# Mixed products of the third contraction tile through the seven-product scheme, low parts of the softmax by pairs of tiles, four heads over eight query tiles

## The chip, the cores and the metric

The kernel runs on one core of one Trainium2 chip. The metric is the device time of one execution in microseconds (us). Three runs before the change took 2610.6 us in the median (2606.59 to 2613.32). The kernel writes its results in float32 and works on float16 pairs: every float32 operand is kept as a high part and a low part (the rest), and a product of two such operands is taken as high x high + high x low + low x high.

## The reference

The reference adds three things: the input x (1 x 2048 x 448, float32), a 16-head attention block of the normalized x, and a mixture of 8 experts in which all 8 are used for every row (so no row is left out, and the gates are a softmax over all 8 logits).

```python
xn = _layernorm(x, axis=-1)
return x + _A_ref(xn, A_wqkv, A_wo) + _B_ref(xn, B_w_gate, B_w1, B_w2)
...
    qkv = (lambda x, *d: x.transpose(*d))((x @ wqkv).reshape(B, S, 3, H, Dh), 2, 0, 3, 1, 4)
    scores = jnp.einsum("bhqd,bhkd->bhqk", q, k) * (Dh ** -0.5)
    p = _softmax(scores, axis=-1)
    o = jnp.einsum("bhqk,bhkd->bhqd", p, v)
...
    for e in range(E):
        w = (gates * mask).sum(-1, keepdims=True)
        h = _silu(xf @ w1[e]) @ w2[e]
        out = out + w * h
```

Here S = 2048, D = 448, H = 16, Dh = 28, E = 8, and the hidden width F of an expert is 1792.

## The kernel before

**Three streams and a planner.** A first stage (phase0, the first 110 us or so) normalizes x, turns it, and makes Q, K, V and the gates. Then two streams run beside each other to the end: the experts (function moe) and the attention (function attention). Nothing is issued directly: every piece of work is a job for one engine, with an estimated duration, a due value v, and the buffers that it reads and writes. Plan.run plays the jobs through with those estimates and issues on each engine, of the jobs that could start, the one with the smallest (v, seq). What comes out is one fixed order of instructions for each engine; on the chip the engines keep that order and wait for each other by semaphores. A buffer tag with n buffers is handed out in the order in which the buffers were asked for.

**Experts.** The 1792 hidden columns of an expert are cut into groups of 5, 5 and 4 tiles of 128: 24 groups in all. The 2048 rows are 4 chunks of 512. For one group and one chunk, unit() makes four hidden tiles (two pairs f = 0, 1; the two pairs are the q of the loops) for two half chunks i = 0, 1 of 256 columns. There are 24 x 4 = 96 units. The contraction over 448 rows has tiles k = 0, 1, 2 of 128 rows and a rest of 64 (k = 3). Tiles 0 and 1 go through a scheme with seven products in place of eight (strassen(), L1084 to L1096): the 2 x 2 blocks of the weights (A) and of x (B) are combined into sums (S1 to S4 in the buffer wa, T1 to T4 in xt). Each product takes three matmuls for each pair (high x high, high x low, low x high), so 7 x 2 x 3 = 42 matmuls of 256 columns. Tile 2, the lone third tile, and the rest are done directly by plain() (L1098 to L1109), four times a unit, with 8 matmuls each: for each pair high x high, high x low and low x high of tile 2 and one for the rest. tails() (L1111 to L1121) adds 8 matmuls that use 64 rows each. The groups of 5 have one further tile (single(), L1162). The second layer is summed() (L1311).

**Attention.** A step is one head and one tile of 128 query rows: 16 x 16 = 256 steps, ordered by TILES: four heads, and for each four query tiles (NB = 4). load_k, load_v and load_q are called once in four steps. In a step, score() multiplies Q by all 2048 keys in two halves (L1420), VectorE takes the extremes (L1424, mx), ScalarE the exponentials (L1437, pf) and the high parts of p (L1445, ph), VectorE the low parts (L1440, pl). turn() transposes both by DMA on SP's queue (L1458: th, tl). weigh() comes once in four steps: lows_of_p() multiplies the low parts of all four tiles by V (L1492), 16 matmuls that use 32 columns of the array each, four beside each other, over 4 x 128 = 512 columns; highs_of_p() does the high parts (L1499). The buffer tl holds four tiles and exists once (TL = 1), th holds one tile and exists four times. project() multiplies by wo (L1585).

Names in the rows: wc holds the high and low parts of tile 2 and the rest; hr holds the high and low parts of the hidden layer; s5 is a copy of a bank in float32 with a buffer of its own, and t (tag th, three buffers) the hidden tile inside silu().

## Time and profile before

| what | value |
|---|---|
| median of three runs | 2610.6 us (2606.59 to 2613.32) |
| the profiled execution, its own time | 2610.42 us |
| its span, first to last instruction | 2608.6 us |
| TensorE busy (PE) | 2572.0 us, 99% |
| VectorE busy (DVE) | 2328.2 us, 89% |
| ScalarE busy (ACT) | 2065.4 us, 79% |
| GpSimd busy (POOL) | 1370.4 us, 53% |
| packets of the DMA queue that SP feeds | 83.7% of 16 engines' span |
| granted TensorE clock, mean | 0.999 |

The profiled execution lies 0.2 us below the median, and 1.8 us of its time lie outside its span. A matmul of TensorE is drawn from its start to its modelled end, and the next one starts well before that end; so the busy share of PE alone does not tell how densely the matmuls follow each other. The distance from one start to the next does.

### The profile page before, as it was taken

The page shows a single profiled execution, that of the slowest core. Times are in us where ns is not written, and L with a number is a line of the kernel's source. Part 1 is how long each engine was busy: PE and PEld are TensorE (multiplying, and loading weights), DVE is VectorE, ACT ScalarE, POOL GpSimd, SP SyncE. Part 2 cuts the span into 40 slices and gives each one's busy share as a digit, 9 for nine tenths or more (in the row PEclk, how much of TensorE's full clock was granted, in tenths as well). Part 3 has the DMA queues.
Part 4 walks back from the last instruction along what each step waited for, and adds up shares of the span by engine and source line. Part 5 has one row for each costly group of instructions (what it writes and reads, how often), then busy time and mean ns, then how long its engine had stood idle before and what let it go on. Part 6 is the DMA issues. An engine that isn't in the chain of part 4 may idle for free.

```text
span 2608.6 us, 54466 instructions
## 1 busy us (share of the span) xinstructions
PE 2572.0 (99%) x20863; PEld 1612.0 (62%) x20863; DVE 2328.2 (89%) x3127; ACT 2065.4 (79%) x2993; POOL 1370.4 (53%) x1377
## 2 busy tenths in 40 slices
PE   9999999999999999999999999999999999999999
PEld 4466666666666666666665666666666666666666
DVE  9689899988998899988999899898889889998986
ACT  5578878886887888778788888888788887878874
POOL 2365545563655545456455556456455653645633
PEclk9999999999999999999999999999999999999999
DMA  9868979887898899968898888877888888997875
GB/s 264 206 153 167 185 173 189 180 174 168 171 195 172 178 175 202 182 155 178 189 182 179 166 189 187 168 177 177 174 177 190 168 172 180 187 197 162 181 157 136
DMA packets 1262757, 466.94 MB, mean 179 GB/s; under 512 B 1169440, under 2 KB 1218080, under 8 KB 1262496
## 3 DMA queue, kind: packets, MB, share of 16 engines
q1 hardware_dynamic: 1261936, 463.44, 83.7%
q8 instruction: 164, 2.69, 0.5%
q14 instruction: 97, 0.79, 0.1%
q10 hardware_dynamic: 560, 0.02, 0.0%
HBM read 160.09 MB, written 17.35 MB: 68 GB/s over the span
## 4 chain that ended last, share of the span: by engine, by line
PE 73%; DVE 14%; ACT 8%; issue 3%; DMA 3%; SPq 0%; DVEq 0%; ACTq 0%
PE banks L1311 29%; PE banks L1090 13%; PE banks L1106 10%; PE banks L1420 7%; PE banks L1162 5%; DVE mx L1424 4%; DVE pl L1440 3%; PE banks L1499 3%; PE banks L1492 2%; ACT pf L1437 2%; ACT ph L1445 2%; DMA tl<-pl 2%; DVE t L1249 2%; PE banks L1117 2%; DVE acc L1322 1%
## 5 line engine op out<-in xcount | busy, mean ns | idle before, releaser
L1311 PE MATMUL banks<-w,hr 128*128 128x448 f16 x5364 | 1083.2, 353 | 2.1 <-DVE t L1249 1.1
L1255 POOL TENSOR_TENSOR hr<-t,hr 128x512 f16<-128x512 f32 x448 | 606.7, 1368 | 576.6 <-ACT hr L1253 553.0
L1437 ACT ACTIVATE pf<-banks,mx 128x1024 f32<-128x1024 f32 x512 | 568.9, 1111 | 322.6 <-DVE mx L1424 316.9
L1311 PEld LDWEIGHTS <-hr 128*128 128x128 f16 x5364 | 516.3, 98 | 493.2 <-issue 24.0
L1440 DVE SCALAR_TENSOR_TENSOR pl<-pf,ph 128x1024 f16<-128x1024 f32 x512 | 718.2, 1404 | 57.2 <-ACT ph L1445 56.6
L1424 DVE TENSOR_REDUCE mx<-banks 128x1 f32<-128x1024 f32 x512 | 622.4, 1216 | 77.0 <-PE banks L1420 60.3
L1445 ACT ACTIVATE ph<-pf 128x1024 f16<-128x1024 f32 x512 | 539.8, 1055 | 6.2
L1090 PEld LDWEIGHTS <-wa 128*128 128x128 f16 x4032 | 392.4, 98 | 115.9 <-issue 13.7
L1106 PE MATMUL banks<-xs,wc 128*128 128x256 f16 x3072 | 395.2, 272 | 1.0 <-DVE banks L1141 0.7
L1106 PEld LDWEIGHTS <-wc 128*128 128x128 f16 x3072 | 299.3, 98 | 61.7 <-issue 5.0
L1246 ACT ACTIVATE t<-banks,the 128x512 f32<-128x512 f32 x448 | 289.8, 683 | 54.2 <-PE banks L1117 38.7
L1249 DVE SCALAR_TENSOR_TENSOR t<-t,banks 128x512 f32<-128x512 f32 x448 | 291.6, 678 | 36.7 <-ACT t L1246 35.7
L1090 PE MATMUL banks<-xt,wa 128*128 128x256 f16 x2304 | 314.4, 272 | 5.4 <-ACT banks L1131 4.7
L1420 PE MATMUL banks<-K,Q 112*128 112x512 f16 x1024 | 306.3, 380 | 2.8 <-ACT pf L1437 2.6
L1253 ACT ACTIVATE hr<-t 128x512 f16<-128x512 f32 x448 | 267.5, 627 | 18.6 <-DVE t L1249 17.9
L1322 DVE SCALAR_TENSOR_TENSOR acc<-banks,gwe,acc 128x448 f32<-128x448 f32 x383 | 254.7, 674 | 30.5 <-PE banks L1311 29.9
L1090 PE MATMUL banks<-xs,wa 128*128 128x256 f16 x1728 | 235.8, 272 | 0.4 <-DVE acc L1322 0.4
L567 POOL TENSOR_TENSOR wc<-r,wc 128x512 f16<-128x512 f32 x64 | 83.6, 1306 | 208.1 <-ACT wc L563 186.0
L634 POOL TENSOR_TENSOR w<-r,w 128x448 f16<-128x448 f32 x112 | 138.5, 1240 | 100.8 <-ACT w L631 94.7
L1162 PE MATMUL banks<-xs,wc 128*128 128x512 f16 x704 | 164.5, 379 | 1.2 <-DVE t L1249 1.2
L1420 PEld LDWEIGHTS <-Q 112*128 112x128 f16 x1024 | 94.4, 98 | 77.3 <-issue 20.8
L1499 PEld LDWEIGHTS <-th 128*128 128x128 f16 x4096 | 118.6, 96 | 13.9 <-issue 4.7
(174 smaller groups left out, 2343.0 us busy)
## 6 DMA issues: line engine op xcount, KB each, us to landing
xt<-xd SPq DMA_DIRECT2D x71, 512.0 KB
K<-qk SPq DMA_DIRECT2D x512, 56.0 KB
r<-in_B_w_dram SPq DMA_DIRECT2D x16, 1120.0 KB
V<-vs SPq DMA_DIRECT2D x64, 256.0 KB
r<-in_B_w_dram SPq DMA_DIRECT2D x16, 960.0 KB
Q<-qk SPq DMA_DIRECT2D x256, 28.0 KB
r<-in_B_w_dram SPq DMA_DIRECT2D x8, 896.0 KB
r<-in_B_w_dram SPq DMA_DIRECT2D x8, 768.0 KB
```

The costliest lines, as they stand in the source:

```text
L1090: nc.tensor.matmul(bank()[:, q * HC : (q + 1) * HC], w, xx, start=(start and q == 0 and i == 0), stop=True, skip_group_check=True,)
L1106: nc.tensor.matmul(bank()[:, q * HC : (q + 1) * HC], ww, xx, start=False, stop=True, skip_group_check=True,)
L1162: nc.tensor.matmul(z(), rows[:, blk, :], xx, start=(i == 0), stop=(i == NTERM - 1))
L1246: add("ACT", 686, lambda: nc.scalar.activation(t(), z(), AF.Tanh, scale=th_()[:, 0:1]), v, r=[z, (th_, 0)], w=[t])
L1249: lambda: nc.vector.scalar_tensor_tensor(t(), t(), 1.0, z(), op0=ALU.add, op1=ALU.mult),
L1255: add("POOL", 1159, lambda: nc.gpsimd.tensor_tensor(hl(), t(), hh(), ALU.subtract), v, r=[t, hh], w=[hl])
L1311: nc.tensor.matmul(y()[:, 0:D], a, wv, start=(i == 0 and u == 0), stop=(i == g - 1 and u == 2))
L1420: nc.tensor.matmul(b()[:, cs], q()[:, q0 : q0 + P], k()[:, cs], start=True, stop=True)
L1424: nc.vector.tensor_reduce(m()[:, n, j : j + 1], b(), op=ALU.min, axis=AX.X)
L1437: nc.scalar.activation(p(), s(), AF.Exp, bias=m()[:, n, j : j + 1], scale=-1.0)
L1440: nc.vector.scalar_tensor_tensor(l()[:, js], p(), P_SCALE, h()[:, js], op0=ALU.mult, op1=ALU.subtract)
L1445: add("ACT", 1060, lambda: nc.scalar.activation(h()[:, js], p(), AF.Copy, scale=P_SCALE), v, r=[p], w=[(h, j)])
```

## The change

**Third tile.** For each output block, the two mixed products of tile 2 are high_f x low_i + low_f x high_i. That is itself a product of a 2 x 2 block matrix of weights, with rows (high_f, low_f), by a 2 x 2 block matrix of x, with rows (low_i, high_i). The change takes it through the same seven products as tiles 0 and 1: every strassen product gets a fourth matmul for each pair, and plain() keeps only high x high and the rest, 4 matmuls in place of 8. The combined blocks of the weights (four of 128 columns for each pair of tiles, scaled by 1 / 2048 on ScalarE, summed on GpSimd) go into wa, which grows from 14 to 18 tiles of 128; those of x are made once on VectorE (first_two, last_two), stored with the other combinations, and loaded with them. xt is now two halves (q) of 6 x 256 with three buffers in place of 8 x 256 with two.

**Low parts of p.** tl is now a ring of two buffers of one tile each. lows_of_p() runs for a pair of tiles: 16 matmuls over 2 x 128 = 256 columns, twice in four steps, each into a bank of its own, and ScalarE copies each bank.

**Order of the steps.** TILES goes through four heads with eight query tiles each (NH = 8), and K and V are loaded once in eight steps. The output tile ost holds eight query tiles.

**Buffers.** s5 now takes one of the three buffers of tag th; the further tile of a group of 5 has its weights in a tag of its own (wz) with one buffer; ro, u and ohl share one; rwo reuses the buffers of rqk; w2 has 8 buffers in place of 7. The planner's rates stay, except UNIT_NS (78 to 76 half rounds).

```diff
-NB, TL, TH = 4, 1, 4
+NB, NH, TL, TH = 4, 8, 2, 4
...
+        add("ACT", 420, less, v, r=[(wc, 0)], w=third)
+        add("POOL", 1150, crosses, v, r=[(wc, 1), *third], w=[(wa, 4)], steps=2)
+        add("POOL", 1150, more_crosses, v, r=[(wc, 1), *third], w=[(wa, 4)], steps=2)
...
-            s5 = buf("mp", [P, C], F32, f"s5{name}", tag="s5")
+            s5 = buf("mp", [P, C], F32, f"s5{name}", tag="th", bufs=RT)
...
-                        for i, (w, xx) in enumerate(((h, xp[0]), (h, xp[1]), (l, xp[0]))):
+                        xx3 = xp[2] if xc is None else xc
+                        for i, (w, xx) in enumerate(((h, xp[0]), (h, xp[1]), (l, xp[0]), (wx, xx3))):
...
-                        for ww, xx in (
-                            (w[:, 0, 0], xs[:, 2, t[i]]), (w[:, 0, 0], xs[:, 6, t[i]]), (w[:, 1, 0], xs[:, 2, t[i]]),
-                            (w[:, 0, 1], xs[:, 3, t[i]]),
-                        ):
+                        for ww, xx in ((w[:, 0, 0], xs[:, 2, t[i]]), (w[:, 0, 1], xs[:, 3, t[i]])):
...
-            XS_[gi, b] = x = buf("mp", [P, 8, HC], F16, f"xt{gi}_{b}", tag="xt", bufs=2)
+            xt = [buf("mp", [P, 6, HC], F16, f"xt{gi}_{b}_{q}", tag="xt", bufs=3) for q in range(2)]
...
-        TILES = [(4 * k + a, t0 + n) for k in range(H // 4) for t0 in range(0, NT, NB) for a in range(4) for n in range(NB)]
+        TILES = [(4 * k + a, t0 + n) for k in range(H // 4) for t0 in range(0, NT, NH) for a in range(4) for n in range(NH)]
...
-                PT[i] = [], buf("ap", [P, NB, NKT, P], F16, f"tl{i}", tag="tl", bufs=TL)
+                PT[i] = [], []
...
+            tl = buf("tl", [P, NKT * P], F16, f"tl{i}", bufs=TL, tag="tl")
...
-            add("PE", 1052, lows_of_p, v, r=[*((tl, q) for q in range(NB)), vb], w=[zl], more=155)
-            add("ACT", 597, lambda: nc.scalar.activation(lt(), zl(), AF.Copy, scale=1 / SEL), v, r=[zl], w=[lt])
+            for u, zl in enumerate(zls):
+                pair = tls[2 * u : 2 * u + 2]
+                add("PE", 560, lambda zl=zl, pair=pair: lows_of_p(zl, pair), v, r=[*pair, vb], w=[zl], more=155)
...
-                load_k(i, 0, at(i - 2) if i else at(-9))
-                load_k(i, 1, at(i - 1))
-                load_v(i, at(i - 2))
+                if i % NH == 0:
+                    load_k(i, 0, at(i - 2) if i else at(-9))
+                    load_k(i, 1, at(i - 1))
+                    load_v(i, at(i - 2))
```

**How the change moves instructions.** On TensorE before, the share of one pair of tiles (one q) of the first of the seven products, in the middle of the program; wa holds the weights, xs the turned x:

```order
L1090 LDWEIGHTS wa_0_15242
L1090 MATMUL banks<-xs,wa_0_15242 128x256
L1090 LDWEIGHTS wa_0_15242
L1090 MATMUL banks<-xs,wa_0_15242 128x256
L1090 LDWEIGHTS wa_0_15242
L1090 MATMUL banks<-xs,wa_0_15242 128x256
```

The same share after; wc holds the parts of the third tile:

```order
L1130 LDWEIGHTS wa_0_15915
L1130 MATMUL banks<-xs,wa_0_15915 128x256
L1130 LDWEIGHTS wa_0_15915
L1130 MATMUL banks<-xs,wa_0_15915 128x256
L1130 LDWEIGHTS wa_0_15915
L1130 MATMUL banks<-xs,wa_0_15915 128x256
L1130 LDWEIGHTS wc_0_16060
L1130 MATMUL banks<-xs,wc_0_16060 128x256
```

One more weight load and matmul of 256 columns, with weights of the third tile, stand at the end of each share. Over the whole program the seven products go from 4032 to 5376 matmuls, and those of plain() from 3072 to 1536.

On TensorE before, the place where a low-part product of four tiles begins; the first rows are the second layer:

```order
L1311 LDWEIGHTS hr
L1311 MATMUL banks<-w_12_1_17435,hr 128x448
L1492 LDWEIGHTS V_17301
L1492 MATMUL banks<-tl_17754,V_17301 32x512
L1492 LDWEIGHTS V_17301
L1492 MATMUL banks<-tl_17754,V_17301 32x512
```

After, the place where a pair's low-part product begins; the first rows are a product of the seven:

```order
L1130 LDWEIGHTS wa_2_15979
L1130 MATMUL banks<-xs,wa_2_15979 128x256
L1574 LDWEIGHTS V_16866
L1574 MATMUL banks<-tl,V_16866 32x256
L1574 LDWEIGHTS V_16866
L1574 MATMUL banks<-tl,V_16866 32x256
```

The matmuls of lows_of_p() have 256 columns in place of 512. They stand in 128 runs of 16 in place of 64 runs of 16, no two runs next to each other, and none of them had to be cut into single tiles of 128 columns.

On SP's queue before, transposes and loads of the steps 100 to 102; tl100 is the one buffer of four tiles, tt the turned result of the low-part product:

```order
L1458 DMA_TRANSPOSE th100_14159<-ph100_14041 128x16x128
L1458 DMA_TRANSPOSE tl100_14211<-pl100_14081 128x16x128
L1509 DMA_TRANSPOSE tt96_14233<-lt96_14220 128x4x128
L388 DMA V104_14269<-vs_73 128x1024
L1458 DMA_TRANSPOSE th101_14311<-ph101_14225 128x16x128
L388 DMA xt10_1_14337<-xd_74 128x2048
L1458 DMA_TRANSPOSE tl100_14211<-pl101_14267 128x16x128
L1458 DMA_TRANSPOSE th102_14405<-ph102_14367 128x16x128
L388 DMA K104_1_14419<-qk_71 28x1024 x4
L1458 DMA_TRANSPOSE tl100_14211<-pl102_14386 128x16x128
```

After, the same steps; tl is the ring of two:

```order
L1536 DMA_TRANSPOSE th100_14242<-ph100_14169 128x16x128
L1598 DMA_TRANSPOSE tt96_14305<-lt96_14049 128x4x128
L1536 DMA_TRANSPOSE tl_1491<-pl100_14295 128x16x128
L390 DMA r2_10_14356<-in_B_w2_dram 128x5x448
L1536 DMA_TRANSPOSE th101_14393<-ph101_14318 128x16x128
L1536 DMA_TRANSPOSE tl_1491<-pl101_14354 128x16x128
L390 DMA xt9_1_1_14458<-xd_74 128x1536
L390 DMA K104_1_14502<-qk_71 28x1024
L1536 DMA_TRANSPOSE th102_14514<-ph102_14433 128x16x128
L390 DMA K104_1_14502<-qk_71 28x1024 x3
L390 DMA xt9_0_0_14565<-xd_74 128x1536
L1536 DMA_TRANSPOSE tl_1491<-pl102_14456 128x16x128
```

Each transpose into tl now goes into the ring, so a transpose of the third tile of four also follows a product that has to set its buffer free. The loads of xt come in halves, and those of K and V half as often: SP issues 1638 DMAs in place of 1829.

## Rows read from the trace of the kernel before

**Rows 1.** The page's head and its first part: busy time, share of the span and instructions of each engine; and the page's fourth part, the shares of the chain of work that ended last.

```profile
span 2608.6 us, 54466 instructions
...
PE 2572.0 (99%) x20863; PEld 1612.0 (62%) x20863; DVE 2328.2 (89%) x3127; ACT 2065.4 (79%) x2993; POOL 1370.4 (53%) x1377
...
PE 73%; DVE 14%; ACT 8%; issue 3%; DMA 3%; SPq 0%; DVEq 0%; ACTq 0%
```

**Rows 2.** Busy time by stretches of 260 us: the first, one in the middle and the last. After the stretch and its length come PE, PEld, DVE, ACT and POOL in us with their instructions, the granted clock, the DMA share and GB/s.

```profile
0.00:260.00 260.00, 250.25 (x1586) 140.22 (x1587) 214.76 (x402) 178.84 (x298) 113.23 (x121) 1.00 0.83 197
...
780.00:1040.00 260.00, 257.75 (x2148) 163.34 (x2146) 236.52 (x306) 213.51 (x304) 141.75 (x145) 1.00 0.88 179
...
2340.00:2608.00 268.00, 263.63 (x2205) 167.61 (x2202) 220.57 (x295) 196.00 (x283) 131.93 (x135) 1.00 0.72 162
```

**Rows 3.** The timeline of PE alone in two pieces around 1003 and 1021 us: start, time from the first start to the last modelled end, line and operation, output and inputs, shape, count of matmuls.

```profile
1003.44 1.04 PE L1106 MATMUL banks<-xs,wc 128*128 128x256 f16 x8
1004.32 0.82 PE L1090 MATMUL banks<-xt,wa 128*128 128x256 f16 x6
1004.97 1.04 PE L1106 MATMUL banks<-xs,wc 128*128 128x256 f16 x8
1005.94 0.61 PE L1117 MATMUL banks<-xs,wc 64*128 64x256 f16 x8
1006.48 1.31 PE L1311 MATMUL banks<-w,hr 128*128 128x448 f16 x6
...
1021.57 1.87 PE L1499 MATMUL banks<-V,th 128*128 128x57 f16 x64
1023.27 0.59 PE L1420 MATMUL banks<-K,Q 112*128 112x512 f16 x2
1023.71 0.82 PE L1090 MATMUL banks<-xt,wa 128*128 128x256 f16 x6
1024.36 0.82 PE L1090 MATMUL banks<-xs,wa 128*128 128x256 f16 x6
1025.02 1.04 PE L1106 MATMUL banks<-xs,wc 128*128 128x256 f16 x8
1025.98 1.05 PE L1492 MATMUL banks<-tl,V 128*32 128x512 f16 x16
1026.96 0.61 PE L1420 MATMUL banks<-K,Q 112*128 112x512 f16 x2
1027.41 1.30 PE L1311 MATMUL banks<-w,hr 128*128 128x448 f16 x6
```

**Rows 4.** Groups by line: the matmuls that the change touches. Count, then busy time in us and mean of one in ns, then PE's idle time before them and what ended it.

```profile
L1106 PE MATMUL banks<-xs,wc 128*128 128x256 f16 x3072 | 395.2, 272 | 1.0 <-DVE banks L1141 0.7 <-DVE the L505 0.3
L1090 PE MATMUL banks<-xt,wa 128*128 128x256 f16 x2304 | 314.4, 272 | 5.4 <-ACT banks L1131 4.7 <-DVE banks L1137 0.2
L1090 PE MATMUL banks<-xs,wa 128*128 128x256 f16 x1728 | 235.8, 272 | 0.4 <-DVE acc L1322 0.4
L1492 PE MATMUL banks<-tl,V 128*32 128x512 f16 x1024 | 67.0, 382 | 7.1 <-DMA tl<-pl 6.5 <-DVE u L1517 0.6
```

**Rows 5.** Waits: who waited for what, total in us, times, the longest.

```profile
PE banks L1492 <- DMA tl<-pl: 6.5, 7, 2.1
PEld L1492 <- DMA tl<-pl: 5.1, 4, 2.4
```

**Rows 6.** Groups by line and shape on ScalarE: the copy of the low-part product over 512 columns, and two copies over 256 and 112.

```profile
L1507 ACT ACTIVATE lt<-banks 128x512 f16<-128x512 f32 x64 | 37.8, 591 | 15.6 <-PE banks L1492 15.4
L586 ACT ACTIVATE wa<-r 128x256 f16<-128x256 f32 x48 | 19.2, 400 | 0.0
L1541 ACT ACTIVATE ost<-os 128x112 f16<-128x112 f32 x64 | 18.5, 289 | 8.5 <-DVE os L1536 8.3
```

**Rows 7.** Groups by line and shape on GpSimd: sums of 128 columns with two inputs, the slowest and the fastest.

```profile
L598 POOL TENSOR_TENSOR r<-r 128x128 f32<-128x128 f32 x48 | 35.1, 732 | 3.8
L597 POOL TENSOR_TENSOR r<-r 128x128 f32<-128x128 f32 x48 | 24.7, 515 | 2.1
```

**Rows 8.** The line of the low parts of p on VectorE: first its own view (count, shortest, median and longest in ns, first and last start in us), then its group (busy time, mean).

```profile
L1440 DVE SCALAR_TENSOR_TENSOR pl<-pf,ph x512: 1205/1224/3096, 142.0 to 2572.4; 128x1024 f16<-128x1024 f32 x171
...
L1440 DVE SCALAR_TENSOR_TENSOR pl<-pf,ph 128x1024 f16<-128x1024 f32 x512 | 718.2, 1404 | 57.2 <-ACT ph L1445 56.6
```

**Rows 9.** DMA: the queue that SP feeds (packets, MB, share of 16 engines), and three of its issues with count and KB each.

```profile
q1 hardware_dynamic: 1261936, 463.44, 83.7%
...
xt<-xd SPq DMA_DIRECT2D x71, 512.0 KB
K<-qk SPq DMA_DIRECT2D x512, 56.0 KB
...
V<-vs SPq DMA_DIRECT2D x64, 256.0 KB
```

More of the change, by code (lines that the diff above doesn't have):

```diff
@@ L335, in issued @@
                 self.have["ap"] = self.ctx.__enter__()
+                self.have["tl"] = Ring(self.have["ap"].tile([P, TL * NKT * P], F16, name="tl"), NKT * P)
     def stop(self):
@@ L659, in phase0 @@
         rv = buf("p0", [P, 4, D + E + 1], F32, "rv")
-        rwo = buf("p0", [HR, 4, D], F32, "rwo")
+        rwo = [buf("p0", [P, 2 * D], F32, f"rwo{k}", tag=f"rqk{k}") for k in range(2)]
         vt = buf("p0", [P, H, TPC, 64], F16, "vt")
@@ L1093, in product @@
                             )
-                keys = [k for w, _ in ws for k in ((w, 0), (w, 1), (w, 2), (w, 3))]
-                xk = xkeys(b) if isinstance(x, tuple) else [(tb, 0), (tb, 1)]
-                return product, 6 * H_NS, [*keys, *xk]
+                keys = [k for w, u in ws for k in (*((w, i) for i in range(5)), (u, 0), (u, 1))]
+                return product, 8 * H_NS, [*keys, *(xkeys(b) if isinstance(x[0], bass.AP) else [(x[0], i) for i in range(3)])]
             def plain(bank, f, i):
@@ L1108, in product @@
                             )
-                return product, 8 * H_NS, [*xkeys(b), *((w, a) for _, w in ws for a in range(2))]
+                return product, 4 * H_NS, [*xkeys(b), *((w, a) for _, w in ws for a in range(2))]
             def tails(ends):
@@ L1129, in unit @@
             last, done, v0 = [], [*lasty], at(spent[0]) - AHEAD
[L1130 removed]
+            v = go([b1], strassen(b1, A11, B11, (0, 0), third[0], start=True))
             add("ACT", 590, lambda: nc.scalar.activation(b2(), b1(), AF.Copy), v, r=[b1], w=[b2])
[L1132 removed]
+            v = go([b3], strassen(b3, S1, T1, 3, start=True))
             add("ACT", 595, lambda: nc.scalar.activation(s5(), b3(), AF.Copy), v, r=[b3], w=[s5])
@@ L1171, in single, with sums_of_x @@
             return lastz
-        def sums_of_x(c, x, v):
+        def sums_of_x(c, xt, v):
+            far = [q for q in range(2) if not xt[q]]
+            xws = []
             for j in range(2):
@@ new lines, in sums_of_x, with pair, first_two @@
+            t = [slice(c * C + i * HC, c * C + (i + 1) * HC) for i in range(2)]
+            def pair(q):
+                if q in far:
+                    o = xws[0]()[:, 8 * P + 2 * q * HC : 8 * P + 2 * (q + 1) * HC]
+                    return o[:, 0:HC], o[:, HC:]
+                return xt[q]()[:, 4], xt[q]()[:, 5]
+            b11, b12, b21, b22 = (xs[:, k, i] for k in (6, 2) for i in t)
+            def first_two():
+                t1, t2 = pair(0)
+                nc.vector.tensor_tensor(t1, b12, b11, ALU.subtract)
+                nc.vector.scalar_tensor_tensor(t2, t1, -LAMBDA, b22, op0=ALU.mult, op1=ALU.add)
@@ new lines, in last_two @@
+            def last_two():
+                t1, t2, t3, t4 = *pair(0), *pair(1)
+                nc.vector.scalar_tensor_tensor(t3, b12, -LAMBDA, b22, op0=ALU.mult, op1=ALU.add)
+                nc.vector.tensor_tensor(t4, b21, t2, ALU.subtract)
+                nc.vector.tensor_scalar(t1, t1, LAMBDA, None, op0=ALU.mult)
+            outs = [(xws[0], "third", q) if q in far else (xt[q], 2) for q in range(2)]
+            add("DVE", 560, first_two, v, r=xkeys(c), w=outs[:1], port=138)
+            add("DVE", 760, last_two, v, r=xkeys(c), w=outs, port=600)
@@ L1223, in sums_of_x @@
+            for q in range(2):
+                dma(
+                    lambda q=q: xd[c, q, :, 4:6],
+                    lambda q=q: xws[0]()[:, 8 * P + 2 * q * HC : 8 * P + 2 * (q + 1) * HC].rearrange("p (k c) -> p k c", k=2)
+                    if q in far else xt[q]()[:, 4:6],
+                    v, r=[outs[q]], w=[("xd", c, q, 2)], kb=128,
                 )
         def sums_x(gi, b, v):
-            XS_[gi, b] = x = buf("mp", [P, 8, HC], F16, f"xt{gi}_{b}", tag="xt", bufs=2)
-            if not gi and b < 2:
-                sums_of_x(b, x, v)
-                return
@@ L1230, in sums_x @@
-            dma(lambda: x(), lambda: xd[b], v, r=[("xd", b, 0), ("xd", b, 1)], w=[(x, 0), (x, 1)], kb=512)
+            near = (2, 1)[b] if not gi and b < 2 else 0
+            xt = [buf("mp", [P, 6, HC], F16, f"xt{gi}_{b}_{q}", tag="xt", bufs=3) for q in range(2)]
+            XS_[gi, b] = xt
+            if near:
+                sums_of_x(b, [x if q < near else None for q, x in enumerate(xt)], v)
+            for q, x in list(enumerate(xt))[near:]:
+                dma(lambda x=x: x(), lambda q=q: xd[b, q], v, r=[("xd", b, q, i) for i in range(3)], w=[(x, i) for i in range(3)], kb=384)
@@ L1486, in apart, with lows_of_p @@
                 nc.scalar.activation(c()[:, 1], c()[:, 0], AF.Copy, scale=SEL)
-            def lows_of_p():
-                for i in range(NKT // 4):
-                    for g in range(4):
-                        kt = g // 2 * (NKT // 2) + 2 * i + g % 2
-                        nc.tensor.matmul(
-                            zl()[32 * g : 32 * (g + 1), 0 : NB * P], vb()[:, kt, DH : DH + 32], tl()[:, :, kt, :],
-                            start=(i == 0), stop=(i == NKT // 4 - 1),
-                        )
+            def lows_of_p(zl, pair):
+                ring = pools.get("tl")
+                a, b = (ring.held[x.name] for x in pair)
+                tl = ring.tile_.rearrange("p (s k q) -> p s k q", s=TL, k=NKT)
+                for n0, ts in [(0, tl[:, a : b + 1 : b - a])] if a < b else [(0, tl[:, a : a + 1]), (1, tl[:, b : b + 1])]:
+                    for i in range(NKT // 4):
+                        for g in range(4):
+                            kt = g // 2 * (NKT // 2) + 2 * i + g % 2
+                            nc.tensor.matmul(
+                                zl()[32 * g : 32 * (g + 1), n0 * P : (n0 + ts.shape[1]) * P], vb()[:, kt, DH : DH + 32],
+                                ts[:, :, kt], start=(n0 == 0 and i == 0), stop=(i == NKT // 4 - 1), skip_group_check=True,
+                            )
             def highs_of_p(n):
```

161 lines of the change are left out of this document (103 added, 58 removed).

## The prediction

> **What bounds the kernel now.** I read the page's first and fourth parts first. PE is busy for 2572.0 of 2608.6 us, DVE for 89%, and the chain that ended last runs through PE for 73% and through DVE for 14% [rows 1]. The stretches say that this is so from end to end: 257.75 of 260 us in the middle, 250.25 in the first stretch, where the attention and the experts have not begun [rows 2]. Busy time alone proves little, so I read starts against starts. A group of six matmuls of 256 columns at 1004.32 is followed by the next at 1004.97, one of eight at 1003.44 by the next at 1004.32: 0.109 us for each matmul, whichever group follows [rows 3]. Most of the program looks like that: PE streams columns without a pause, and what ends last is nearly always PE itself. So the price of an edit is first the number of columns that PE streams, then what PE has to wait for newly; work on DVE, ACT, POOL and the queues counts where it makes PE late.
>
> **Switches of the array.** Two kinds of products use part of the array, and rows 3 show what they cost beyond their columns. The eight matmuls of L1106 at 1025.02 should end their issue at 1025.89 (8 x 0.109); the low parts of p (L1492) start at 1025.98, and the next product at 1026.96. From 1025.89 that is 1.07 us. Two matmuls of 512 columns of L1420 take 0.44 us (1023.27 to 1023.71), so four rounds of 512 columns are worth 0.88 us. 0.19 us are left, half ahead of the run (1025.89 to 1025.98) and half behind it. L1117, with four rounds of 256 columns, says the same: from 1005.84 (1004.97 + 8 x 0.109) to 1006.48 are 0.64 us, of which 0.436 are columns and 0.20 switching [rows 3].
>
> **The change part by part.**
>
> Third tile on PE: plain() had 3072 matmuls, the seven products 4032 [rows 4]. With a fourth matmul in each share of three the products come to 4032 x 4/3 = 5376, plain() halves to 1536. 7104 become 6912, all of 256 columns: 192 x 0.109 = -20.9 us, all of it on the path.
>
> Low parts of p: 64 runs of 16 matmuls with 512 columns (1024) [rows 4] become 128 runs with 256. The columns stay the same; the switches double, as no two runs stand next to each other. A run of four rounds with 256 columns is bounded by the nearest one, L1117 with two pieces of the array: 0.64 us. So 128 x 0.64 - 64 x 1.07 = 81.9 - 68.5 = +13.4 us. The other end: a round here has four weight loads in 0.109 us, which no row shows. A load and a matmul of 57 columns on the whole array follow each other every 1.70 / 64 = 0.027 us (1021.57 to 1023.27) [rows 3], and four such loads just fit. If a load took twice that, a round would take 0.215 us, and 512 rounds 512 x 0.106 = 54 us more. I take the first value, since L1492 as it is loads four times in each round and shows nothing beyond columns and switches.
> On this the Trainium skill is worth weighing ("TensorE: Matmul & The Clock Gate", Part 3, The mechanism): it says that a weight load overlaps a running matmul only when the row group differs. The four pieces of L1492 use all rows, so by this rule its four rounds would show their loads on top of the columns; the trace shows 0.19 us beside the columns for the whole run and 0.20 for L1117, whose loads do differ in rows, so it does not agree. By the page's figure for a load (columns / 1.2, so 27 ns for 32, in LDWEIGHTS), 256 more rounds with four exposed loads would be an estimated 256 x 0.107 = 27 us. That is the third rival below, priced there from rows.
>
> Waits of PE for the low parts: now PE waits 6.5 us for tl in 7 of 64 runs, its weight loads 5.1 us in 4 more [rows 5]. With 128 runs these could be twice as many, +6.5 to +11.6 us; or none more, since K and V come half as often and SP's queue is freer, or fewer, down to -6.5. The matmuls that stand between a pair's last score product and its run, priced by the distances of rows 3, are worth 16.5 us in the median after and 16.3 before: the margin stays, the chances to miss it double. I take +3 us, the half of PE's own.
>
> ScalarE: 64 copies of 591 ns become 128 of 256 columns. Between 400 (256 columns) and 289 ns (112) I take 390: 49.9 - 37.8 = +12 us; 48 scaled copies at 400 ns are +19 us [rows 6]. 2065.4 becomes about 2097 us, 80%: beside PE, taken at 0.
>
> GpSimd: 192 sums of 128 columns at 515 to 732 ns [rows 7] are +99 to +141 us, 53% becomes 57 to 58%. They share access to the buffers with DVE, and that is not free: the low parts of p take 1205 ns at their shortest and 1404 in the mean, (1404 - 1205) x 512 = 102 us for 1370 us of GpSimd [rows 1, 8]; so +7 to +10 us on DVE. Its own new work is small: 20 sums of 256 columns in the first 130 us. DVE goes from 89% to 90%. PE has the experts to do while a step of the attention is late, so I take 0, with +10 as the bound.
>
> DMA: K 512 x 56 KB and V 64 x 256 KB halve (-22.5 MB); xt goes from 71 x 512 to 143 x 384 KB (+18.6 MB), of 463.44 MB [rows 9]. Next to nothing, and SP issues 191 DMAs fewer. xt's second half waits for a buffer until the third of the seven products, a whole unit ahead of its use: 0.
>
> Buffers shared (s5 in the ring of t, one buffer for the further tile): no row shows their waits. A ring of three with five hidden tiles and one s5 in a unit of some 26 us (2500 us for 96 units) leaves each holder 13 us; I take 0, bounds 0 to +6.
>
> Sum: -20.9 + 13.4 + 3 = -4.5 us. The profiled execution took 2610.42 us, 0.2 below the median, so 2605.9; I predict 2606.
>
> **The rivals.** A measurement of this kernel tells a change from none at about 0.3%, 7.8 us: below 2602.8 or above 2618.4.
>
> The gain is kept whole (22%). For it: with eight steps for each K and V the attention needs less of SP, and in the order of PE the matmuls behind the last score product are worth 77 us after against 37 before. Now the last low part of p starts at 2572.4 us of 2608.6 [rows 8], so the attention ends with the kernel, and its delays have nothing to hide behind at the end. If the waits for tl go away as well: 2610.4 - 20.9 + 13.4 - 6.5 = 2596. Against it: that wait is a matter of when a transpose lands, and the margin is unchanged.
>
> The ring of two makes PE wait (18%). Each transpose into tl must wait until the run of the pair ahead has freed its buffer, now every two steps, and what stands behind it on SP's queue (th of the next step, K, Q, xt) waits too, so a late run makes the next run late. PE's mean wait is 6.5 / 7 = 0.93 us [rows 5]. With 7 of 64 runs it decides nothing; the gain of 7.5 us is eaten when (7 + 8) of 128 wait, and with a third of them (43) waiting it is 43 x 0.93 - 6.5 = +33.5, so 2610.4 - 7.5 + 33.5 = 2636; with a quarter 2626. I put 2626. Against it: the planner holds a transpose back until its buffer is free in its own account, and so plans for that wait.
>
> The weight loads don't fit into half rounds (5%). By a quarter of the bound above, 54 / 4 = 13.5 us: 2619; by the whole 2660.
>
> The change does not bring its columns through because DVE or the ring of t becomes the bound (6%): +10 and +6 us: 2622.
>
> **How the numbers follow.** The forecast has the other 49%, with its own range 2598 to 2613. About a third of it lies below 2602.8, and nearly all of the first rival: 0.16 + 0.21 = 0.37 faster. Slower takes most of the other three: 0.16 + 0.03 + 0.04 = 0.23, less what of them stays below 2618.4, 0.22. The same: 0.41. The range reaches down to 2589, the first rival with some 7 us of PE's 36.6 us of idle time [rows 1] gone as well, and up to 2630, a little over the ring rival's price; beyond lie the dearest loads and the third of runs waiting.
>
> **What would show it.** In the profile after: matmuls of the strassen line 5376 and of the plain line 1536, still 0.109 us apart; each low-part run 0.64 us from the end of its neighbour's columns to the next start, not 1.07 (that is the weight-load rival); PE's wait for tl near 10 us over 128 runs, not 6 and not 30; the low parts of p on VectorE near 1420 ns in the mean; GpSimd at 57%. PE's busy time should fall by about 8 us. I am wrong if the waits for tl pass 20 us, if the run takes over 0.75 us, or if PE waits for xt, wa or a bank of the experts in places where it did not.

## The result, and the profile after

The changed kernel takes 2630.2 us in the median (2623.1 to 2634.0), the kernel before 2610.6: a ratio of 1.0076 (95%: 1.0055 to 1.0096), 20 us slower, where 2606 was predicted and 2630 was the end of the range. The profiled execution took 2627.5 us.

The page's head, first part and chain of the kernel after:

```profile
span 2625.7 us, 56188 instructions
...
PE 2573.4 (98%) x21695; PEld 1613.4 (61%) x21695; DVE 2344.0 (89%) x3149; ACT 2078.9 (79%) x3105; POOL 1487.7 (57%) x1569
...
PE 69%; DVE 17%; ACT 6%; DMA 4%; issue 3%; POOL 1%; SPq 0%; DVEq 0%; ACTq 0%; POOLq 0%
```

Against [rows 1], GpSimd came out at the share predicted, VectorE and ScalarE a per cent below; but PE's busy time, which was to fall by 8 us, rose by 1.4, and the chain has moved from PE (73 to 69%) to VectorE (14 to 17%). First, did PE get the work that was promised? The lines of the matmuls (count; shortest, median and longest ns; first and last start):

```profile
L1130 PE MATMUL banks<-xt,wa x2880: 269/273/418, 124.6 to 2604.4; 128*128 128x256 f16 x192
L1130 PE MATMUL banks<-xs,wa x1920: 270/273/421, 123.7 to 2602.7; 128*128 128x256 f16 x192
...
L1130 PE MATMUL banks<-xs,wc x384: 272/273/421, 124.1 to 2600.5; 128*128 128x256 f16 x192
L1130 PE MATMUL banks<-xt,wc x192: 272/273/273, 142.1 to 2604.5; 128*128 128x256 f16 x192
...
L1142 PE MATMUL banks<-xs,wc x1536: 269/272/421, 129.6 to 2604.9; 128*128 128x256 f16 x192
```

The four groups of L1130 make 5376, L1142 has 1536: 6912 in place of the 7104 of [rows 4]. The timeline of PE, around one run of the low parts of p:

```profile
1008.73 0.49 PE L1130 MATMUL banks<-xt,wa 128*128 128x256 f16 x3
1009.06 0.27 PE L1130 MATMUL banks<-xt,wc 128*128 128x256 f16 x1
1009.17 0.49 PE L1130 MATMUL banks<-xt,wa 128*128 128x256 f16 x3
...
1013.53 0.60 PE L1496 MATMUL banks<-K,Q 112*128 112x512 f16 x2
1014.43 0.62 PE L1574 MATMUL banks<-tl,V 128*32 128x256 f16 x16 [0.30 <-DVE t L1325]
1014.98 2.82 PE L1387 MATMUL banks<-w,hr 128*128 128x448 f16 x14
```

Four matmuls from 1008.73 to 1009.17 are 0.11 us each, as in [rows 3]. The run of 16 takes 0.55 us from its start to the next (0.436 of columns); with the switch ahead, the 128 runs cost 0.65 us each in the median, predicted 0.64, and show nothing of their weight loads. So the work is there, or rather gone. What came in its place stands in the waits of PE (total, times, longest):

```profile
PE banks L1496 <- ACT pf L1513: 12.3, 19, 2.5
PE banks L1574 <- DMA tl<-pl: 8.1, 8, 2.2
PE banks L1130 <- DVE banks L1173: 6.5, 4, 4.9
PE banks L1387 <- ACT lt L1592: 2.6, 4, 1.4
```

The wait for tl, which the prediction feared most, is 8.1 us, 1.6 more than in [rows 5]. The top row is new in its size: the next score product (L1496) needs a bank that the exponentials (pf) have read. Before, that wait was

```profile
PE banks L1420 <- ACT pf L1437: 2.6, 7, 0.7
```

The stretches (columns as in rows 2):

```profile
0.00:260.00 260.00, 240.09 (x1513) 130.96 (x1513) 214.72 (x415) 171.33 (x288) 109.03 (x125) 0.97 0.82 199
...
120.00:180.00 60.00, 48.34 (x310) 29.15 (x308) 41.73 (x68) 37.21 (x57) 26.04 (x28) 0.89 0.73 164
```

and before, for the second of them:

```profile
120.00:180.00 60.00, 58.55 (x407) 37.92 (x405) 45.86 (x68) 44.26 (x67) 30.62 (x31) 1.00 0.75 163
```

10 of the first stretch's 260 us that were busy before [rows 2] are idle, all of it between 120 and 180, and there the granted clock falls from 1.00 to 0.89. The timeline of that place, all engines but the DMA issues left out:

```profile
133.18 0.31 POOL L1451 MEMSET ost<- 128x256 f16 x1 [4.89 <-DMA qk<-ql]
133.45 1.15 POOL L1240 TENSOR_TENSOR xt<-xs,xt 128x512 f16<-128x512 f32 x1
...
134.64 0.60 ACT L1169 ACTIVATE s<-banks 128x512 f32<-128x512 f32 x1 [4.09 <-POOL xt L1240]
135.27 0.70 DVE L1173 TENSOR_TENSOR banks<-banks,s 128x512 f32<-128x512 f32 x1 [4.05 <-ACT s L1169]
136.02 1.22 PE L1130 MATMUL banks<-xt,wa 128*128 128x256 f16 x5 [4.94 <-DVE banks L1173]
```

Each of the last three brackets names the row above: a clearing of ost on GpSimd waits for a DMA, the sums of x behind it on GpSimd end late, s5 (L1169) needs the buffer of the ring of t that those sums hold, and PE stands 4.94 us. Then PE alone:

```profile
136.02 1.86 PE L1130 MATMUL banks<-xt,wa 128*128 128x256 f16 x8 [4.94 <-DVE banks L1173]
137.68 1.91 PE L1130 MATMUL banks<-xs,wa 128*128 128x256 f16 x8
...
148.60 1.01 PE L1496 MATMUL banks<-K,Q 112*128 112x512 f16 x2 [2.53 <-ACT pf L1513]
```

Eight matmuls take 1.66 us in place of 0.87: the lower level of TensorE's clock (1.2 GHz of 2.4), right after PE stood.

I added up over all of PE's starts what a distance to the next start exceeds the usual one for its shape, apart where the clock was low. This splits each span (some 10 us of each, at its two ends, are in none of the columns); all rows are worked out so from the profiled executions, in us:

| kernel | span | PE's work | lost to the lower clock | standing |
|---|---|---|---|---|
| before | 2608.6 | 2550.6 | 1.7 | 46.0 |
| after | 2625.7 | 2543.9 | 9.6 | 62.1 |
| e4, pairs alone | 2622.6 | 2565.1 | 3.3 | 44.2 |
| e7, third tile alone | 2636.9 | 2530.0 | 14.1 | 82.8 |
| e13, before with fewer columns | 2599.2 | 2529.9 | 1.7 | 57.3 |
| e11, before in another order | 2632.6 | 2551.0 | 6.4 | 65.7 |
| e2, s5 in its own buffer | 2614.6 | 2544.1 | 4.6 | 56.0 |

PE's work fell by 6.7 us (predicted 7.5 without waits); 8 us of lower clock and 16 us of standing came back, some 10 of the 16 in the first 260 us. The split hangs on what is taken as usual: taken for each pair of neighbouring shapes, the level of PE's work is some 60 us lower in every row, and from before to after it falls by 4.4, the lower clock rises by 7.5 and the standing by 15.0. So differences between rows are good to some 3 us.

### The profile page after: what moved, and what is told of

Its sections match the earlier page's. It is cut to its first block, busy times and chain, and to the rows that moved or that the text cites. A ratio compares the mean times of both kernels' runs of the same rounds, so it can differ in the third digit from the quotient of the medians.

```text
span 2625.7 us, 56188 instructions
## 1 busy us (share of the span) xinstructions
PE 2573.4 (98%) x21695; PEld 1613.4 (61%) x21695; DVE 2344.0 (89%) x3149; ACT 2078.9 (79%) x3105; POOL 1487.7 (57%) x1569
## 4 chain that ended last, share of the span: by engine, by line
PE 69%; DVE 17%; ACT 6%; DMA 4%; issue 3%; POOL 1%; SPq 0%; DVEq 0%; ACTq 0%; POOLq 0%
PE banks L1387 28%; PE banks L1130 17%; PE banks L1496 6%; PE banks L1142 5%; PE banks L1198 5%; DVE pl L1516 4%; DVE mx L1500 4%; PE banks L1581 3%; PE banks L1574 2%; DVE t L1325 2%; DMA tl<-pl 2%; ACT pf L1513 2%; PE banks L1153 1%; DVE acc L1398 1%; ACT ph L1521 1%
## 5 line engine op out<-in xcount | busy, mean ns | idle before, releaser
L1331 POOL TENSOR_TENSOR hr<-t,hr 128x512 f16<-128x512 f32 x448 | 613.6, 1383 | 564.5 <-ACT hr L1329 539.9
L1516 DVE SCALAR_TENSOR_TENSOR pl<-pf,ph 128x1024 f16<-128x1024 f32 x512 | 729.5, 1427 | 28.3 <-ACT ph L1521 27.1
L1130 PEld LDWEIGHTS <-wa 128*128 128x128 f16 x4800 | 467.4, 98 | 133.7 <-issue 17.7
L1130 PE MATMUL banks<-xt,wa 128*128 128x256 f16 x2880 | 388.3, 273 | 8.9 <-DVE banks L1173 6.5
L1496 PE MATMUL banks<-K,Q 112*128 112x512 f16 x1024 | 306.6, 380 | 12.8 <-ACT pf L1513 12.3
L1130 PE MATMUL banks<-xs,wa 128*128 128x256 f16 x1920 | 280.3, 274 | 0.0
L1142 PE MATMUL banks<-xs,wc 128*128 128x256 f16 x1536 | 227.1, 273 | 0.5 <-DVE banks L1177 0.3
L1142 PEld LDWEIGHTS <-wc 128*128 128x128 f16 x1536 | 148.4, 98 | 44.1 <-issue 5.7
L1496 PEld LDWEIGHTS <-Q 112*128 112x128 f16 x1024 | 95.3, 98 | 79.2 <-issue 25.2
L1581 PEld LDWEIGHTS <-th 128*128 128x128 f16 x4096 | 119.1, 96 | 16.4 <-issue 4.0
```

Of the source, the lines that this page charges most:

```text
L1130: nc.tensor.matmul(bank()[:, q * HC : (q + 1) * HC], w, xx, start=(start and q == 0 and i == 0), stop=True, skip_group_check=True,)
L1142: nc.tensor.matmul(bank()[:, q * HC : (q + 1) * HC], ww, xx, start=False, stop=True, skip_group_check=True,)
L1331: add("POOL", 1159, lambda: nc.gpsimd.tensor_tensor(hl(), t(), hh(), ALU.subtract), v, r=[t, hh], w=[hl])
L1496: nc.tensor.matmul(b()[:, cs], q()[:, q0 : q0 + P], k()[:, cs], start=True, stop=True)
L1516: nc.vector.scalar_tensor_tensor(l()[:, js], p(), P_SCALE, h()[:, js], op0=ALU.mult, op1=ALU.subtract)
```

## The experiments

Ratios are to the kernel before, run on the same chip (2606.2 to 2611.2 us there); us beside them are the ratio's distance from 1 times 2610.6, and kernels of different chips are compared by them. The letters in the expectations name theories in the order in which they came up; those that decided are G, H and J, at e13 to e15. One letter changes its meaning: at e9 and e11, G is the rival that the work added on other engines makes the waits (from e13 on this is H), and what is called F there, that the pace of the attention decides, is G from e13 on.

**The pairs, and the third tile, each alone.** e4 is the kernel before with the ring of two and the 128 runs; e7 the kernel after with whole runs, four query tiles, the further tile's weights back in the ring of wc, and six buffers of w2 (they pay for tl); e8 is e7 with s5 in a buffer of its own and five of w2.

```diff
-NB, TL, TH = 4, 1, 4
+NB, TL, TH = 4, 2, 4
...
+            tl = buf("tl", [P, NKT * P], F16, f"tl{i}", bufs=TL, tag="tl")
...
```

> Kernel before with the low parts of p by pairs in a ring of two, and nothing else of the change. PE's switches are worth 128 x 0.646 - 64 x 1.073 = +14 us by the two traces. Theory A: that and about 3 us of waits, 2625 to 2630. Theory C: the ring of two also makes PE wait for the low parts all along, by 9 us or more beyond the switches: 2633 or more. If the pairs cost less than their switches: under 2622.

Measured 1.0062 (1.0050 to 1.0074; +16 us).

```profile
PE 2586.7 (99%) x21887; PEld 1629.6 (62%) x21887; DVE 2335.8 (89%) x3127; ACT 2072.5 (79%) x3057; POOL 1379.9 (53%) x1377
```

PE's busy time rises by 14.7 us over [rows 1]; VectorE and ScalarE rise by 7 to 8 us, GpSimd by 10, and PE's waits for tl by 2.4 us, to 8.9. So the time is that of the switches, as worked out; what theory C wanted, 9 us of waits beyond them, did not come.

```diff
-NB, NH, TL, TH = 4, 8, 2, 4
-RWA, RWC, RWZ, RW2, RH, RT, RPF = 4, 4, 1, 8, 8, 3, 2
+NB, NH, TL, TH = 4, 4, 1, 4
+RWA, RWC, RWZ, RW2, RH, RT, RPF = 4, 4, 1, 6, 8, 3, 2
...
```

> Changed kernel without the pairs and without the eight-tile order: the low parts of p go four tiles at a time through one buffer of four tiles, and the order is four query tiles for each head, as before the change; to make room the further tile's weights are back in the ring of wc, and w2 has 6 buffers. The third tile's scheme and s5 in the ring of t stay. Theory D: -20.9 us of columns, +8 to +11 for s5: 2594 to 2600. Theory E: 2602 or more.

> As the run with the third tile alone, but s5 has its own buffer again, and w2 has 5 buffers to make room. Theory D: the columns alone, -20.9 us, less what fewer buffers for w2 cost (0 to 6 us): 2585 to 2592. Theory E: 2598 or more. If w2 with 5 buffers makes PE wait at each change of the group (23 times), 2600 or more with waits for the second layer's weights in the trace.

Measured 1.0134 (1.0120 to 1.0148; +35 us) and 1.0143 (1.0128 to 1.0158). In e7 PE's work falls by 20.6 us, as predicted, and the kernel is slower than with the pairs; both runs lie far beyond theory D, and agree with theory E, which set no upper end. The waits of e7:

```profile
PE banks L1495 <- ACT pf L1512: 28.6, 24, 2.9
PE banks L1567 <- DMA tl<-pl: 7.6, 7, 2.7
PE banks L1129 <- DVE banks L1172: 6.0, 7, 2.2
```

The attention tells why. VectorE's low parts of p, in e4 and in e7 (first and last start):

```profile
L1441 DVE SCALAR_TENSOR_TENSOR pl<-pf,ph x512: 1204/1226/2230, 144.5 to 2550.0; 128x1024 f16<-128x1024 f32 x171
```

```profile
L1515 DVE SCALAR_TENSOR_TENSOR pl<-pf,ph x512: 1204/1226/2250, 145.4 to 2550.7; 128x1024 f16<-128x1024 f32 x171
```

2405.5 and 2405.3 us, although e7 gives PE 35 us less to do. Here PE doesn't set the attention's length; what it saves goes into standing, and into experts left over behind the attention (2636.9 - 2550.7 = 86 us against 36 before). Work left over is no loss by itself: e4 leaves 2622.6 - 2550.0 = 73 us behind, and PE waits 2.5 us for pf there, as before.

**The start.** e1 puts the clearing of ost behind the last sums of x.

```diff
...
-        add("POOL", 200, lambda: nc.gpsimd.memset(ost()[:, :, :, HR:P], 0.0), at(-20), w=[(ost, "pad")])
+        add("POOL", 200, lambda: nc.gpsimd.memset(ost()[:, :, :, HR:P], 0.0), at(-20), w=[(ost, "pad")], after=xlow)
```

> Changed kernel with one edit: GpSimd's small fill of ost's pad is put behind its last sum of x's combinations (before, it stood there by itself). Theory A (most of the loss is made at the start: the fill waits for the last store of q and k, the sum of x behind it on GpSimd is late, the buffer of the ring of t that it reads stays held, the copy s5 that now takes its buffer from that ring is late, PE stands for about 5 us and its clock falls to half): PE's wait for L1173's bank near 131 us shrinks from 5 us to under 1.5, the clock stays at full speed in the first 260 us, and the time falls by 10 to 15 us, to 2615 to 2620. Theory B (the shared ring of t costs all along the program) and theory C (the ring of two for the low parts costs all along): the start gains little, under 5 us; 2625 or more.

Measured 1.0080 (1.0068 to 1.0093). The longest of those waits halves, to 2.2 us in place of the 1.5 expected, but the time stays, against theory A: the clearing is a cause of the stall at 136 us, and shortening that stall gave nothing back.

```profile
PE banks L1131 <- DVE banks L1174: 4.1, 5, 2.2
```

**s5 in the ring of t.** e2 gives s5 its own buffer again, for one of w2; e6 puts s5 into the ring in the kernel before.

```diff
-RWA, RWC, RWZ, RW2, RH, RT, RPF = 4, 4, 1, 8, 8, 3, 2
+RWA, RWC, RWZ, RW2, RH, RT, RPF = 4, 4, 1, 7, 8, 3, 2
...
-            s5 = buf("mp", [P, C], F32, f"s5{name}", tag="th", bufs=RT)
+            s5 = buf("mp", [P, C], F32, f"s5{name}", tag="s5")
```

> Changed kernel with s5 in a buffer of its own again, as before the change; to make room w2 has 7 buffers in place of 8, as before the change. Theory A: the copy s5 does not wait for the ring any more, the start gains as in the run with the fill moved: 2615 to 2620, and the stalls behind 260 us stay near 43 us. Theory B: the stalls behind 260 us fall too, to the 35 us of the kernel before: 2605 to 2612. Theory C: only the start could change, by under 5 us.

> Kernel before with one edit: s5 takes its buffer from the ring of t (three buffers), as in the changed kernel. Theory D (the loss is the switches and waits of the pairs, +17, and s5 in the shared ring with the falls of the clock behind its stalls, +11): 2614 to 2619, with PE's waits for the score bank (behind ScalarE's exponentials) up from 3 us to 8 or more. Theory E (sharing is cheap by itself; what costs is the added work of the third tile on ScalarE and GpSimd): within 3 us of the kernel before.

Measured 1.0033 (1.0020 to 1.0045; 11 us less than after) and 1.0026 (1.0014 to 1.0039; +7 us). In e2 PE's waits at the seven products drop out of the first rows, and those for the exponentials halve:

```profile
PE banks L1496 <- ACT pf L1513: 6.3, 13, 1.0
PE banks L1574 <- DMA tl<-pl: 5.3, 7, 1.7
```

In e6 the waits for the exponentials rise from 2.6 us, as theory D has it, with a time between D and E:

```profile
PE banks L1420 <- ACT pf L1437: 8.7, 15, 2.0
```

Both edits also move the planned order: e6 leaves 2611.1 - 2544.5 = 67 us behind the attention (before 36), e2 50 (after 73). So the 7 and 11 us are those of the edit with the order that follows from it.

**The third tile's own sums.** e14 is e2 without the 48 scaled copies and 192 sums; the fourth matmuls take other weights, so PE has the same work and the output is another.

```diff
-        add("ACT", 420, less, v, r=[(wc, 0)], w=third)
-        add("POOL", 1150, crosses, v, r=[(wc, 1), *third], w=[(wa, 4)], steps=2)
-        add("POOL", 1150, more_crosses, v, r=[(wc, 1), *third], w=[(wa, 4)], steps=2)
...
-                            wx = wa[:, (14 + cross) * P : (15 + cross) * P]
+                            wx = wc[:, cross * P : (cross + 1) * P]
...
```

> The changed kernel with s5 in a buffer of its own (e2, 2615.2 us), without the third tile's own preparation: no scaled copy on ScalarE (48), no sums on GpSimd (192); the fourth matmul of each share takes a piece of the plain weights instead. Left out of the computation: the mixed products' weights are wrong ones; TensorE has the same matmuls. Theory H (the added work delays the attention through ScalarE's queue and VectorE's access to the buffers): 2595 to 2605 us. Theories G and J: within 5 us of e2, 2610 to 2620 us.

Measured 0.9995 (0.9985 to 1.0004): 10 us less than e2. (The 2609.6 us stand beside 2611.2 for the kernel before on this chip, where e2's stand beside 2606.2; at that level it would be 2605, the upper end of theory H; as measured, it lies between H and the others.) VectorE's low parts of p in e2 and in e14 (busy, mean):

```profile
L1516 DVE SCALAR_TENSOR_TENSOR pl<-pf,ph 128x1024 f16<-128x1024 f32 x512 | 732.6, 1433 | 44.3 <-ACT ph L1521 41.9 <-DMA tl<-pl 1.6 <-issue 0.2
```

```profile
L1513 DVE SCALAR_TENSOR_TENSOR pl<-pf,ph 128x1024 f16<-128x1024 f32 x512 | 718.8, 1406 | 46.3 <-ACT ph L1518 44.6 <-ACT pf L1510 1.2
```

14 us of VectorE go with GpSimd's sums and ScalarE's copies, and the time falls by 10. PE's waits in e14:

```profile
PE banks L1571 <- DMA tl<-pl: 11.1, 10, 2.2
PE banks L1493 <- DMA K<-qk: 5.5, 1, 5.5
...
PE banks L1493 <- ACT pf L1510: 1.3, 4, 0.4
```

The wait for the exponentials has gone from 6.3 us to 1.3, although e14 leaves more behind the attention (2610.2 - 2547.7 = 62.5 us) than e2 (50.3). Work left over doesn't explain that; the sums and copies, which the edit takes away, can, though which of the two was not tried apart. What remains is elsewhere: a wait of 5.5 us for K at the start of the attention, waits for tl, and a granted clock of 0.996 in the mean.

**Columns alone.** e13 leaves one matmul out of each share of the bank b4 in the kernel before: 192 matmuls, the third tile's number, and no work is added. The planner is told of it, with the same UNIT_NS as in the change, so the order moves a little. (It is the first of the four, a plain product, not a mixed one as the expectation says; the columns are the same.)

```diff
-                        ):
+                        )[f & i :]:
...
-    UNIT_NS = 78 * H_NS + 200
+    UNIT_NS = 76 * H_NS + 200
```

> The kernel before, from which two matmuls of 256 columns are left out of each unit of the experts (one of the mixed products of the bank b4, in each of its two shares): 192 matmuls, 20.9 us of columns, the number that the third tile saves, with no other work, no other buffer. Left out of the computation: that product. TensorE's work in a step of the attention falls from 9.45 to 9.39 us by the order. Theory G (VectorE and ScalarE hold the step of the attention at 9.4 us, and TensorE's freed time comes back as waits and half speed): at least half of the 20.9 us is lost, 2599 to 2612 us. Theories H and J (columns come through where nothing else is changed): 2587 to 2593 us.

Measured 0.9962 (0.9948 to 0.9977): 10 of 20.9 us, as theory G has it. Two rows hold most of what is lost. The first was 2.6 us in 7 before; the second has no like before: PE waits once, at the very end, for the attention's output.

```profile
PE banks L1420 <- ACT pf L1437: 7.5, 10, 1.9
...
PE banks L1585 <- DMA ohl<-ost: 3.6, 1, 3.6
```

**The order.** LEAD sets how early the attention ends by the plan. e11 sets it to 200 in the kernel before (no instruction changes, only places); e9 to 30 in the kernel after; e10 and e12 to 40 in e7 and e8; e16 to 80 in e2. e15 leaves 5 of the 7 buffers of w2 in the kernel before, e5 ends the experts' plan 5 us later, e3 goes back to four query tiles.

```diff
-M_AT, A_AT, LEAD, END, LAND, TURN = 60.0, 0.0, 130.0, 2585.0, 3500, 4500
+M_AT, A_AT, LEAD, END, LAND, TURN = 60.0, 0.0, 200.0, 2585.0, 3500, 4500
```

> Kernel before with LEAD at 200, no work changed: 9.30 us worth of matmuls in a step in place of 9.45, and 77 us worth behind the last score product in place of 38. Theory F: the kernel before is made slower by the order alone, to 2612 to 2625, with PE's wait for the exponentials up from 3 us to 10 or more. Rival G: within 5 us of the kernel before.

> Changed kernel with the planner's constant LEAD at 30 in place of 130, and no other edit: the attention's due values are spread over more of the program, so the order of PE puts 9.46 us worth of matmuls into a step in place of 9.27 (matmuls counted in the order, priced by the distances of the trace before), and 29 us worth behind the last score product in place of 77. Theory F (in nine traces the attention's step takes 9.40 to 9.52 us whatever PE has to do, with VectorE at 91%; an order that puts less than that into a step makes PE stand at the score bank, and what PE did not do meanwhile is left for the end, where it runs alone): PE's wait for the exponentials falls from 12 us to under 6, the stretch behind the last low part of p from 72 to about 35 us, and the time to 2600 to 2610. Rival G (the waits come from the work itself that the change adds on ScalarE, GpSimd and the shared ring): within 6 us of the changed kernel, 2620 or more.

> The kernel before with 5 buffers for w2 in place of 7, no other edit; by the order TensorE's work in a step of the attention falls from 9.45 to 9.33 us and what stands behind the last score product grows from 38 to 68 us. Theory J (the buffers of w2 decide the order, and the order decides the time): slower by 10 to 30 us, 2620 to 2640, with waits of TensorE for the exponentials at a bank of the scores above 10 us. Theory H: the same as before, 2605 to 2612 us.

> The changed kernel with s5 in a buffer of its own (e2, 2615.2 us) and the constant that sets how early the attention ends by the plan at 80 in place of 130 us; by the order TensorE's work in a step of the attention rises from 9.356 to 9.384 us. Theory G (the pace decides): 2605 to 2612 us, waits for the exponentials at a bank of the scores below 6 us. Theories H and J: within 4 us of e2, 2611 to 2619 us.

| run | ratio | 95% | us to before |
|---|---|---|---|
| e11 before, LEAD 200 | 1.0119 | 1.0106 to 1.0132 | +31 |
| e15 before, 5 buffers of w2 | 1.0037 | 1.0023 to 1.0052 | +10 |
| e9 after, LEAD 30 | 1.0050 | 1.0039 to 1.0062 | +13 |
| e16 s5 own, LEAD 80 | 1.0012 | 1.0000 to 1.0024 | +3 |
| e10 third alone, LEAD 40 | 1.0098 | 1.0085 to 1.0111 | +26 |
| e12 the same, s5 own | 1.0062 | 1.0049 to 1.0075 | +16 |
| e5 after, END 2590 | 1.0078 | 1.0065 to 1.0091 | +20 |
| e3 after, four tiles | 1.0080 | 1.0064 to 1.0095 | +21 |

e11 is the plainest case: the same work on every engine, and 31 us. Its waits and its low parts of p:

```profile
PE banks L1420 <- ACT pf L1437: 15.1, 14, 3.5
```

```profile
L1440 DVE SCALAR_TENSOR_TENSOR pl<-pf,ph x512: 1206/1225/2217, 141.2 to 2556.1; 128x1024 f16<-128x1024 f32 x171
```

The 31 us are more than theory F allowed (2612 to 2625). With more of the experts placed behind the attention (76 us, before 36), PE has less to do between two score products and reaches the bank before the exponentials do. Buffers of w2 do the same: e15 leaves 2618.4 - 2553.6 = 65 us behind (its low parts of p start last at 2553.6) and waits 8.6 us for pf, not over 10. That is theory J in its direction, at its lower end. But pace is not all: e16 is 5 us below e2 by its ratio, with intervals that overlap, and misses theory G's 2605 to 2612 with 2616; it still waits 10.0 us for pf, not under 6. e9 misses theory F's 2600 to 2610 with 2621: it waits 12.7 us, as much as after, and is 7 us faster with less left behind (34 us, its last low part of p starting at 2585.6, for 73). e10 and e12 were expected at 2580 to 2600 by the same theory and took 2633 and 2624. No version with the third tile and its sums beats the kernel before; e16, the best of them, can't be told from it.

## Why the prediction was wrong, point by point

**The third tile, -20.9 us "all of it on the path".** PE's work fell by just that (e7, e13: 20.6 and 20.7), but this is the step that failed first. In e13, where no work is added, half of it reaches the end. I took the rows of an even stretch as proof that PE sets the pace everywhere; they prove that PE was just busy enough. The attention's low parts of p run from 142.0 to 2572.4 before [rows 8], from

```profile
L1516 DVE SCALAR_TENSOR_TENSOR pl<-pf,ph x512: 1204/1256/3080, 147.3 to 2552.5; 128x1024 f16<-128x1024 f32 x171
```

after. The 17 us of span are +5.3 ahead of the attention, -25.2 in it (2430.4 to 2405.2) and +37.0 behind (36.2 to 73.2). The prediction counted 77 us of matmuls behind the last score product against 37 and read that for the rival "the gain is kept whole". It was the other way: PE's work within the attention falls by some 37 + 6.7 us, the attention by 25, and most of the difference is standing and lower clock. What the third tile did is plainest against e4, which has the same pairs, the same length of the attention (2405.5 us) and as much behind it (72.6): PE's work is 21.2 us less after, and 17.9 us of standing and 6.3 of lower clock stand in its place. Beside the columns this holds the sums, s5 in the ring and the eight-tile order. The prediction also took the first 260 us for a stretch in which the attention and the experts have not begun; the low parts of p start at 142.0 [rows 8], and some 10 us of the loss are made between 120 and 180. One sign that it named for being wrong came: PE waits for a bank of the experts, 6.5 us behind VectorE at the seven products, where it was 0.2 [rows 4]; 4.9 of it are the stall at 136 us.

**The runs by pairs, +13.4.** Right: 0.65 us for a run, +14.5 us of PE's work and +16 us of time alone (e4); with the +3 for tl, 16.4 had been the sum. The rival of the weight loads is out: nothing of the 54 us. The rule weighed there, from the page "TensorE: Matmul & The Clock Gate" of the Trainium skill (Part 3, The mechanism), does not hold for these loads: by it and the page's figure for a load the runs would have been dearer by an estimated 27 us.

**Waits for tl, +3.** 8.1 us after, 1.6 more; predicted about 10. So the rival of the ring of two (18%) is wrong in its mechanism, although its 2626 us lies nearest to the time.

**GpSimd, ScalarE and VectorE, taken 0, bound 10.** The sizes were right: POOL 57%, the low parts of p 1427 ns (predicted near 1420), copies of

```profile
L1592 ACT ACTIVATE lt<-banks 128x256 f16<-128x256 f32 x128 | 48.5, 379 | 42.2 <-PE banks L1574 36.5 <-DVE pl L1516 2.1 <-POOL ost L1635 1.4
L622 ACT ACTIVATE r<-wc 128x256 f32<-128x256 f16 x48 | 19.9, 414 | 0.7 <-POOL wc L569 0.7
```

49 and 20 us. ScalarE's total is 2078.9 us, not 2097: the 31 us of new work came, and its other work fell by 17 us, for a reason that was not looked for. The choice of 0 was wrong: e14 puts the bound, 10 us, in its place. "PE has the experts to do while a step of the attention is late" fails because PE takes its work in a fixed order; what stands behind a waiting score product waits with it.

**Shared buffers, taken 0, bounds 0 to +6.** s5 in the ring, with the order that follows from it, costs 7 us in the kernel before (by its interval 4 to 10) and 11 in the one after, above the bound. e12 against e10 says 9 us; e8 against e7 says nothing was gained, but each pays with one buffer of w2. e15 leaves as much behind the attention as e6 (65 and 67 us), waits as long for pf (8.6 and 8.7) and loses as much (10 and 7 us) without touching s5, so how much is the ring and how much the order stays open. "13 us for each holder" is a mean; at the start the sums of x hold the ring and wait for GpSimd.

**Together.** From after, s5's own buffer takes 11 us (e2) and leaving out the sums another 10 (e14): 21 of the 20 that were lost. Then PE's own saving of 7.5 has shrunk to about 1 (0.9995). Edits moved the planned order too, and an order alone can be worth 31 us (e11), so the parts are not pure; the wait that vanishes in e14 is the best sign that the sums are a cause of their own. That the rival of VectorE and the ring (6%) named the two terms, 10 and 6 us, was right, and its chance far too small.

**Open.** The third tile alone loses more than its parts: 35 us, where half of the columns (-10), s5 (+7 to +11), the sums (+10) and fewer buffers of w2 (up to +10, e15) make 17 to 21. With the plan's end moved, e12 still loses 16. Why PE stands so often there has not been separated from the order that the plan gives it.

## What to carry to other kernels

Busy at 99% and evenly spaced starts show that an engine is the bound now, not that it stays one by 0.8% less: look at how busy the next engine is in the stage that counts (here VectorE and ScalarE in the attention), and take what a cut saves on the first engine for an upper bound there (here 10 of 20.9 us came through). VectorE is busy for 91% of the stretch from 260 to 2340 us before, ScalarE for 81%; that it is VectorE that holds the attention's length was argued, not shown. When an order written by a planner leaves more work behind the last step of the slower chain, see whether the engine that does it has enough left beside that chain (e4 has and loses nothing by it, e11 has not); vary the constant that paces it before judging the edit. A helper engine's work and a shared buffer are not free when the path runs through a second engine.

## What the hardware showed that I had not expected

That standing costs twice. Before, the granted clock is 0.999 in the mean; after

```profile
core 0: 2625.7 us, clock 0.995
```

or 0.9954 before rounding, which is some 2 x 0.46% x 2626 = 24 us at 1.2 GHz, and by the starts 9.6 us lost. Stalls of 4.9 us (ahead of 136.02) and of 2.5 us (148.60) have matmuls at the low level behind them; in e7 it is 14 us with 29 us of waits for pf, in e13 no more than before, with 7.5 us of such waits. And an order alone, with no instruction changed, moves this kernel by 1.2% (e11), more than the change under study.
